# A replanned opening: ScalarE scales half of one attention unit, fillers move to free banks, and a transposition passes four loads

## The chip, the cores and the metric

The program runs on one core of a Trainium2 chip. The metric is the device time of one execution in microseconds (us), as the median of several runs. The engines are named as the profile names them: PE (TensorE, matmuls; PEld its weight loads), DVE (VectorE), ACT (ScalarE), POOL (GpSimd) and SP (SyncE, which here only issues transfers). "PEq" or "SPq" is the part of an engine that issues.

## The reference

Retention attention, then a two-layer feed-forward network with an ELU between the layers. There is no routing, although the weights are called moe.

```python
# q, k, v: (8 batches, 8 heads, 576 rows, 64), float32
scores = scale * np.matmul(q, k.transpose(0, 1, 3, 2))          # scale = 1/8
gamma = 1.0 - 2.0 ** (-5.0 - np.arange(H))
Dmat = np.where(rel >= 0, gamma[:, None, None] ** rel, 0.0)     # rel = row - column
attn = np.matmul(scores * Dmat, v)
x = attn.transpose(0, 2, 1, 3).reshape(4608, 512)               # heads side by side
h = x @ w_in                                                    # (512, 2048)
g = np.where(h > 0.0, h, np.exp(np.minimum(h, 0.0)) - 1.0)
out = g @ w_out                                                 # (2048, 512), float32 out
```

The decay is split into a factor for each query row (gamma to the power of its position, with the scale) and one for each key row (gamma to minus its position). So q and k are multiplied by small tables first, and the scores need only a mask of zeros and ones.

## The kernel before

**Units.** Rows 0 to 511 of every batch are cut into four units: two halves of 256 rows, each for heads 0 to 3 and for heads 4 to 7. Unit n is batch n // 4, so units 0 to 3 are batch 0, and unit 3 is its second half of rows with heads 4 to 7. Rows 512 to 575 of four batches at a time form a tail unit. A unit goes through these operations, which carry the names below in the code:

- `ldq`, `ldk`, `ldv`: loads of 256 KB, issued by SP (L422). From unit 8 on each is two loads of 128 KB (`ldq0_10`: queries of unit 10, first half; L412).
- `cq`, `ck` (L494): scaling of queries or keys by their table, with a cast to bf16, in two halves each. In a name like `ck13` the first digit is the half and the rest is the unit: second half of the keys of unit 3. `cv` (L545) casts the values.
- `T` and `cp` (L558, L564): PE transposes the scaled queries, then the keys, into PSUM, and ACT or DVE copies them out. From unit 7 on a transposing transfer from SP does this instead: `tr` (L602), which waits for the scaling of its unit.
- `sc`, `mask`: score matmuls, then the mask on DVE (L937; L931 from unit 8). `st`, `mid`, `end`, `bm`, `be`: the state (keys times values), running sums of it and their block-diagonal forms (L803 to L834), which later units of the batch read. `iv`: the unit's output, from states and from masked scores. `xc` copies it out as transposed tokens `xt` (L993). From unit 5 on one step `S` does the output of the unit or pair before and the scores and states of the next; `Sout7` is the output of unit 7 alone.

**Feed-forward.** Tokens are taken in blocks of 256 (blocks 0 to 5), later of 512. `F1_b_p` is a step of 8 matmuls of block b with w_in into one PSUM bank; then `ex` (Exp on ACT, L1145), `md` (max with 0 on ACT or DVE, L1153 or L1155) and `g` (on DVE, L1160) make the ELU, and `g` lets go of the bank. `F2_b_i_c` multiplies with w_out, over several steps into one bank, which `oc` (L1200) copies out after the last of them. There are six such banks (tag `f`) and two more for the scores. States and outputs of the units take banks from the same six.

**Weights.** w_in and w_out come in four pieces each, `wi0` to `wi3` and `wo0` to `wo3` (L471, L479), issued by POOL, which casts them to bf16 on the way. SP and POOL issue into two queues that share the 16 DMA engines. The loads of unit 4 are held back: a small memset of POOL into the buffer of its queries (`hold4`, L431) stands behind `wi0`, and `ldq4` waits for it.

**Order.** The order of all operations is not written out. At build time a planner (`Plan.run`) plays the program through with a cost for each operation on each engine it may run on, a rank, the dependencies and the numbers of buffers, and gives each engine one list, which then runs in that order. Constants steer it: `ON` fixes an operation to an engine, `RANKS` shifts a rank, `LAG` is an extra delay that the planner gives to transfers in a stretch of the opening. Where it finds PE idle in the first 50 us, the emitting loop at the end puts matmuls on a tile of zeros ahead of the next operation (fillers, L1341 to L1354), into that operation's own bank; ahead of a `T` they are transposes.

Of the kernel before, what the change touches and what calls it, by code (L numbers as in the profile page):

```python
# [11 lines left out]
FP32 = mybir.dt.float32  # L12
# [5 lines left out]
P = 128  # L18
# [6 lines left out]
class Op:  # L25


    def __init__(self, name, cost, deps, emit, rank, take=(), use=(), banks=(), dma=None, after=None):
        self.name, self.cost, self.emit, self.rank = name, cost, emit, rank
        self.deps = [d for d in deps if d is not None]  # L30
        self.turn = [] if after is None else [after]
        self.take, self.use, self.banks, self.dma = take, [*use, *(t[1] for t in take)], banks, dma
        self.eng = self.start = self.end = self.done = None
        self.slot, self.waits, self.at, self.side = {}, [], 0.0, False


class Plan:
# [30 lines left out]
    def run(self, began):  # L68
# [4 lines left out]
        bank, lanes = {}, {"SP": 0, "POOL": 0, "ACT": 0}  # L73
        wire = {"SP": [], "POOL": [], "ACT": []}
        free, order, events = dict(began), [], []
        ready, lack, next_of = {e: [] for e in began}, {}, {}
        for op in self.ops:
            lack[op] = len(op.deps) + len(op.turn)
# [48 lines left out]
        while len(order) < len(self.ops) or any(wire.values()) or events:  # L127
            again = True
            while again:
                again = False  # L130
                for e in began:
                    if free[e] > now + 1e-9:
                        continue
                    best = pick(e, now)
                    if best is None:
                        continue
                    _, op, got = best
                    for o in op.cost:
                        ready[o].remove(op)
                    cost = op.cost[e]  # L140
                    pay = cost[0] if isinstance(cost, tuple) else cost
                    if op.side and e in BESIDE and now + 0.15 < busy.get(BESIDE[e][0], 0.0):
                        pay += BESIDE[e][1]
                    if op.side:
                        busy[e] = now + pay
                    op.eng, op.start, op.end = e, now, now + pay - (LAP[e] if op.dma is None else 0.0)
                    op.done = None
                    op.waits = [*op.deps, *(bank[b] for b in op.banks if b in bank and bank[b].eng != e)]
                    for b in op.banks:
                        bank[b] = op  # L150
                    op.slot = {}
                    for key, (cls, n) in got.items():
                        if self.slots[cls][n] is not None:
                            op.waits += self.users[self.slots[cls][n]]
                        self.slots[cls][n], op.slot[key] = key, n
                    free[e] = op.end
                    heapq.heappush(events, (op.end, next(count), None))
                    if op.dma is None:
                        heapq.heappush(events, (op.end + HOP[e], next(count), op))
                    else:  # L160
                        lanes[e] += 1
                        enter = now + (op.dma[2] if len(op.dma) > 2 else ENTER)
                        heapq.heappush(events, (enter, next(count), None))
                        wire[e].append([enter, op.dma[0], op, False])
                    order.append(op)
                    met(op, "begun")
                    again = True
            heads = {e: w[0] for e, w in wire.items() if w and w[0][0] <= now + 1e-9}
            big = [e for e, h in heads.items() if h[3] and len(h[2].dma) > 2]
            heads = {e: h for e, h in heads.items() if h[3] or big in ([], [e])}  # L170
            for h in heads.values():
                h[3] = True
            turn = {e: h[2].dma[0] / h[2].dma[1] for e, h in heads.items()}
            rate = {e: turn[e] / sum(turn.values()) for e in heads}
            step = min([h[1] / rate[e] for e, h in heads.items()], default=1e9)
            assert events or heads, [o.name for o in self.ops if o not in set(order)][:20]
            if events:
                step = min(step, events[0][0] - now)
            step = max(step, 0.0)
            now += step  # L180
            for e, h in heads.items():
                h[1] -= step * rate[e]
                if h[1] < 1e-6:
                    wire[e].pop(0)
                    lanes[e] -= 1
                    heapq.heappush(events, (now + LEAVE + (LAG if LAG_AT < now < LAG_TO else 0.0), next(count), h[2]))
            while events and events[0][0] <= now + 1e-9:
                _, _, op = heapq.heappop(events)
                if op is not None:
                    finish(op, now)  # L190
# [3 lines left out]
ENTER, LEAVE = 1.25, 0.55  # L194
PIECE = 4.3
SEQ = "q0 k0 v0 q1 k1 v1 q2 k2 v2 q3 k3 v3"
LAG, LAG_AT, LAG_TO = 1.5, 11.3, 46.0


LEAD = 64  # L200
HOLD = {4: "wi0"}
RANKS = {}
TOGETHER = 1
EARLY = 5
LOOSE = True
# [3 lines left out]
POOL0 = 3.6  # L209
MERGE = {}  # L210
FROM = (8.96, 10.28, 13.13, 15.23, 17.0, 17.0, 17.44, 17.82)
ON = {'mid1': 'DVE', 'be2': 'DVE', 'md_1_0': 'ACT', 'xc1_2': 'DVE', 'cv0': 'DVE', 'md_1_1': 'ACT', 'cq12': 'DVE'}
DIRECT = True
PAIR = 8
FAR = 8
# [26 lines left out]
def kernel(  # L242
# [32 lines left out]
    def mm(*a, **kw):  # L275
        return pin(nc.tensor.matmul(*a, **kw))  # L276
# [209 lines left out]
    def scaled(it, i, e, cost):  # L486
        n = it.n
        key, raw = ("qkn", n), ("rq" + "qk"[i], n)
        g = ((far_q, far_k) if it.far else (gq, gk))[i]
        g = g[:, 2 * it.T + e, 4 * it.w : 4 * it.w + 4].unsqueeze(2).to_broadcast([P, 4, D])  # L490

        def emit(op):
            dst = by_head(n)[:, i, :, e] if it.far else tiles[key][:, i, e]
            pin(alu[op.eng].tensor_tensor(dst, tiles[raw][:, :, e], g, ALU.mult))  # L494

        first = not hasattr(it, "cq")
        if first:
            it.cq = {}
        ready = [it.ld["qk"[i], e], far_ready[0]] if it.far else [it.ld["qk"[i]]]
        op = add(f"c{'qk'[i]}{e}{n}", cost, ready, emit, it.rank,  # L500
                 take=[T("qkn", key, [P, 2, 2, 4, D], BF16)] if first else [], use=([] if first else [key]) + [raw],
                 after=it.cq0 if not first else None)
        if first:
            it.cq0 = op
        it.cq[i, e] = op
# [70 lines left out]
    def prepare(it, turn):  # L576
        n = it.n
        if it.early:
            qc, kc = {"DVE": 0.44, "POOL": 0.62}, {"POOL": 0.62, "DVE": 0.44}
            vc = {"ACT": 0.62, "POOL": 0.65, "DVE": (0.42, 0.3)}  # L580
        else:
            qc = kc = {"POOL": 0.64, "DVE": (0.6, 1.5)}
            vc = {"POOL": 0.65, "ACT": (0.62, 1.0)}
# [724 lines left out]
                        ffn2(blk, it, c, 4, rank + 8 * it + 2 * c, n0, n1)  # L1308

    for op in plan.ops:  # L1310
        op.side = len(op.cost) > 1 and op.name[:2] in ("cq", "ck", "ct", "cv", "bm", "be")
    named = {op.name: op for op in plan.ops}
    for op, name in holds:
        op.deps.append(named[name])
# [5 lines left out]
    for name, e in ON.items():  # L1320
        if name in named and e in named[name].cost:
            named[name].cost = {e: named[name].cost[e]}
    for name, shift in RANKS.items():
        if name in named:
            named[name].rank += shift
# [2 lines left out]
        PRINT(order)  # L1328
        return

    last = 1.3
    for op in order:
        for cls, key, shape, dt in op.take:
            pool = psum if cls in ("f", "sc") else sbuf
            if cls == "z":
# [2 lines left out]
                tiles[key] = put_aside(cls, op.slot[key], shape)  # L1338
            else:
                tiles[key] = pool.tile(shape, dt, name=cls, tag=f"{cls}{op.slot[key]}")  # L1340
        if op.eng == "PE":  # L1341
            gap = op.start - last if op.start < 50 and op.take else 0.0
            if gap > 0:
                spot = tiles[op.take[0][1]]
                left = int(gap * 0.8 / (0.107 if op.start < 7.0 else 0.056))
                while left > 0:
                    if op.name.startswith("T"):
                        wide = 1
                        pin(nc.tensor.transpose(spot[:, left % 4], zero[:, :P], ident))
                    else:  # L1350
                        wide = min(left, 4)
                        mm((spot if len(spot.shape) == 2 else spot[:, 0])[:, : wide * P], zero[:, :P],
                           zero[:, : wide * P], start=True, stop=True)
                    left -= wide  # L1354
            last = op.end
        op.emit(op)


# [31 lines left out]
```

## Time and profile before

| | |
|---|---|
| Three runs | 298.35, 298.99, 299.23 us; median 298.99 |
| The profiled execution | 299.29 us, of which the span from the first instruction to the last is 297.6 |
| PE busy | 291.7 us, 98% of the span |
| ACT, DVE, POOL busy | 195.1, 179.7, 136.5 us |
| First matmul of the feed-forward | at 18.91 us |
| First use of queries, keys and values of unit 4 by POOL | at 30.77, 34.33 and 37.99 us |
| First matmul of step `S7` | at 58.35 us |

Times of single instructions are counted from the start of the span. An engine runs its list in order, so an instruction that waits holds up all that stands behind it.

### The profile page before, as it was taken

The page shows a single profiled execution, that of the slowest core. Times are in us where ns is not written, and L with a number is a line of the kernel's source. Part 1 is how long each engine was busy: PE and PEld are TensorE (multiplying, and loading weights), DVE is VectorE, ACT ScalarE, POOL GpSimd, SP SyncE. Part 2 cuts the span into 40 slices and gives each one's busy share as a digit, 9 for nine tenths or more (in the row PEclk, how much of TensorE's full clock was granted, in tenths as well). Part 3 has the DMA queues.
Part 4 walks back from the last instruction along what each step waited for, and adds up shares of the span by engine and source line. Part 5 has one row for each costly group of instructions (what it writes and reads, how often), then busy time and mean ns, then how long its engine had stood idle before and what let it go on. Part 6 is the DMA issues. An engine that isn't in the chain of part 4 may idle for free.

```text
span 297.6 us, 8887 instructions
## 1 busy us (share of the span) xinstructions
PE 291.7 (98%) x3560; PEld 164.4 (55%) x3560; DVE 179.7 (60%) x323; ACT 195.1 (66%) x383; POOL 136.5 (46%) x257
## 2 busy tenths in 40 slices
PE   7999999999999999999999999999999999999996
PEld 3678746867776664545545454545444544444445
DVE  5999935838755849697756556666550169643300
ACT  2449823859768758778696868676772289777512
POOL 5880379956856755666534558542444000000000
PEclk9999999999999999999999999999999999999999
DMA  7999999999999999999999999996497410011132
GB/s 207 260 206 204 216 280 217 219 174 200 193 194 187 196 189 204 193 237 200 208 222 298 208 219 203 196 189 161 103 169 172 90 39 1 0 39 35 35 106 73
DMA packets 142010, 50.14 MB, mean 168 GB/s; under 512 B 120720, under 2 KB 137488, under 8 KB 141968
## 3 DMA queue, kind: packets, MB, share of 16 engines
q1 hardware_dynamic: 137744, 45.37, 78.3%
q0 software_dynamic: 4224, 4.19, 8.6%
q8 instruction: 28, 0.46, 0.7%
q14 instruction: 14, 0.11, 0.1%
HBM read 36.70 MB, written 9.44 MB: 155 GB/s over the span
## 4 chain that ended last, share of the span: by engine, by line
PE 86%; DMA 7%; POOL 3%; DVE 2%; SPq 1%; issue 0%; ACT 0%; ACTq 0%
PE f L276 84%; DMA rv<-in_v_dram 7%; PE sc L276 2%; POOL w_out_sb L479 1%; DVE pt L937 1%; SPq L422 1%; POOL w_in_sb L471 1%; POOL s_end L820 0%; POOL qkn L494 0%; DVE qkn L494 0%; PE f L558 0%; DVE s_end L820 0%; DVE s_mid L834 0%; POOL s_mid L820 0%; POOL vn L545 0%
## 5 line engine op out<-in xcount | busy, mean ns | idle before, releaser
L276 PE MATMUL f<-w_out_sb,g 128*128 128x512 bf16 (+2 forms) x608 | 141.1, 368 | 0.0
L276 PE MATMUL f<-xt,w_in_sb 128*128 128x256 bf16 (+1 forms) x768 | 138.2, 326 | 0.0
L1160 DVE SCALAR_TENSOR_TENSOR g<-e,f 128x512 bf16<-128x512 f32 x144 | 95.9, 684 | 69.0 <-ACT f L1153 53.2
L1145 ACT ACTIVATE e<-f 128x512 f32<-128x512 f32 x144 | 84.8, 597 | 33.7 <-PE f L276 25.7
L276 PEld LDWEIGHTS <-w_in_sb 128*128 128x128 bf16 x768 | 74.7, 98 | 53.5 <-DVE xt L988 0.4
L276 PEld LDWEIGHTS <-g 128*128 128x128 bf16 x608 | 56.6, 98 | 57.9
L1153 ACT ACTIVATE f<-f 128x512 f32<-128x512 f32 x116 | 68.5, 593 | 0.0
L494 POOL TENSOR_TENSOR qkn<-rqk,far_q 128x256 bf16<-128x256 f32 x48 | 28.9, 614 | 9.2 <-DMA rqk<-in_q_dram 9.0
L494 POOL TENSOR_TENSOR qkn<-rqk,far_k 128x256 bf16<-128x256 f32 x48 | 29.0, 616 | 7.6 <-DMA rqk<-in_k_dram 7.2
L1200 ACT COPY ot<-f 128x512 f32<-128x512 f32 (+2 forms) x30 | 16.8, 560 | 19.9 <-PE f L276 19.9
L545 POOL CAST vn<-rv 128x512 bf16<-128x512 f32 x28 | 17.1, 612 | 21.7 <-DMA rv<-in_v_dram 16.6
L972 ACT CAST xt<-f 128x512 bf16<-128x512 f32 x24 | 12.9, 589 | 16.1 <-PE f L276 16.1
L877 POOL CAST y<-mid 64x256 bf16<-64x256 f32 x36 | 14.3, 401 | 19.8 <-DVE mid L862 10.4
L1155 DVE TENSOR_SCALAR f<-f 128x512 f32<-128x512 f32 x28 | 19.4, 694 | 1.0 <-ACT e L1145 0.7
L931 DVE TENSOR_TENSOR pt<-sc,mask_t 128x1024 bf16<-128x1024 f32 x12 | 14.6, 1220 | 2.4 <-PE sc L276 2.4
L618 POOL TENSOR_TENSOR aside<-aside,gq 128x256 bf16<-128x256 f32 x16 | 9.4, 614 | 11.3 <-DMA aside<-in_k_dram 11.2
L494 POOL TENSOR_TENSOR qkn<-rqk,gq 128x256 bf16<-128x256 f32 x13 | 8.1, 633 | 12.3 <-DMA rqk<-in_q_dram 12.3
L877 ACT CAST y<-mid 64x256 bf16<-64x256 f32 x30 | 11.6, 402 | 2.1 <-DVE mid L860 1.0
L862 DVE TENSOR_TENSOR mid<-f,mid 128x256 f32<-128x256 f32 x24 | 10.2, 424 | 2.8 <-PE f L276 0.5
L276 PE MATMUL f<-pt,vn 64*64 64x64 bf16 (+1 forms) x512 | 11.5, 202 | 0.2 <-DVE pt L937 0.2
L993 ACT CAST xt<-f 128x256 bf16<-128x256 f32 x10 | 4.2, 452 | 10.8 <-PE f L276 10.8
L937 DVE TENSOR_TENSOR pt<-sc,mask 128x1024 bf16<-128x1024 f32 x8 | 9.8, 1220 | 2.2 <-PE sc L276 2.1
(92 smaller groups left out, 172.7 us busy)
## 6 DMA issues: line engine op xcount, KB each, us to landing
rqk<-in_q_dram SPq DMA_DIRECT2D x48, 128.0 KB, 3.9
rqk<-in_k_dram SPq DMA_DIRECT2D x48, 128.0 KB, 3.5
rv<-in_v_dram SPq DMA_DIRECT2D x48, 128.0 KB, 3.4
out_dram<-ot SPq DMA_DIRECT2D x18, 256.0 KB, 3.5
out_dram<-ot SPq DMA_DIRECT2D x19, 128.0 KB, 2.4
rqk<-in_q_dram SPq DMA_DIRECT2D x8, 256.0 KB, 6.8
rqk<-in_k_dram SPq DMA_DIRECT2D x8, 256.0 KB, 5.8
rv<-in_v_dram SPq DMA_DIRECT2D x8, 256.0 KB, 5.9
```

Source lines behind the costliest of these rows:

```text
L276: return pin(nc.tensor.matmul(*a, **kw))
L494: pin(alu[op.eng].tensor_tensor(dst, tiles[raw][:, :, e], g, ALU.mult))
L545: pin(copy[op.eng](tiles["vn", n], tiles["rv", n]))
L877: pin(copy[op.eng](dst, tiles[key][j * D : (j + 1) * D]))
L931: pin(nc.vector.tensor_tensor(tiles[it.pt].rearrange("p i h n -> p (i h n)")[:, : 2 * w * C].rearrange("p (i x n) -> p i x n", i=2, n=C), ...
L937: pin(nc.vector.tensor_tensor(tiles["pt", n].rearrange("p i h n -> p (i h) n"), tiles[it.sc].rearrange("p i (h n) -> p (i h) n", h=2), mas ...
L972: pin(copy[op.eng](by_block(it.xt)[:, 2 * it.T + c], tiles[xkey, c].rearrange("p (h n) -> p h n", n=P)))
L1145: pin(nc.scalar.activation(tiles[ekey], tiles[hkey], AF.Exp))
L1153: pin(nc.scalar.activation(ph, ph, AF.Relu))
L1155: pin(nc.vector.tensor_scalar_max(ph, ph, 0.0))
L1160: pin(nc.vector.scalar_tensor_tensor(tiles[gkey], tiles[ekey], -1.0, tiles[hkey], ALU.add, ALU.min))
L1200: pin(copy[op.eng](tiles[okey][:, :cols], tiles[pkey][:, :cols]))
```

## The change

Nothing that is computed changes. In the opening ACT takes four operations of unit 3, and some of the planner's rules and constants are changed, so that the lists of all engines differ in places.

- `cq13` and `ck13`, on POOL before, run on ACT, as four instructions each, one per head (a multiplication by a factor per partition). `ck03` goes from DVE to POOL, `cp(3, 0)` and `xc0_3` from DVE to ACT, `be3` from POOL to DVE, `md_0_1` from ACT to DVE.
- POOL's list is then: `bm2`, `ck03`, `wi3`, `wo0` to `wo3`, `hold4`. Before it was: `bm2`, `cq13`, `wi3`, `ck13`, `wo0` to `wo3`, `be3`, `hold4`.
- PE's list in the opening is: `T(3, 0)`, `T(3, 1)`, `iv2`, `sc3`, `st3`, first feed-forward step. Before: `T(3, 0)`, `iv2`, `T(3, 1)`, `st3`, `sc3`, first feed-forward step.
- Fillers go into whichever of the six banks has been free longest, ahead of any idle stretch that is planned, and never as transposes: 23 matmuls of up to 512 columns, 65 instructions before.
- `ldq0_10` may not go before `tr7`. SP's list there is: `ldv1_9`, `tr7`, the four loads of queries and keys of unit 10, `tr8`. Before: `ldv1_9`, those four loads, `tr7`, two loads of values and one of unit 11, `tr8`.
- PE's list from 56 us on: `S7` stands ahead of `F1_2_7`, and the last step `F2_2_0_3` of its bank stands behind `F1_3_3`; before it stood ahead of `F1_3_0`. `md_3_1` goes from ACT to DVE, ahead of `mask8`. Before `F1_3_4`, both lists hold the same steps.
- Later, neighbours change places in a few spots, and about 35 small operations change between ACT, DVE and POOL.

```diff
@@ Plan.run
                     if op.side and e in BESIDE and now + 0.15 < busy.get(BESIDE[e][0], 0.0):
-                        pay += BESIDE[e][1]
-                    if op.side:
-                        busy[e] = now + pay
+                        pay = max(pay, busy["POOL"] - now + 0.3) if e == "DVE" else pay + BESIDE[e][1]
+                    if op.side or e == "POOL" and op.dma is not None:
+                        busy[e] = now + (pay if op.side else 0.45)
...
+                    if e == "PE" and now < 50 and now > last + 0.01 and not op.name.startswith("F"):
+                        free_f = [(self.freed.get(old, 0.0), n, self.users.get(old, [])) for n, old in enumerate(self.slots["f"])
+                                  if old is None or self.left[old] == 0]
+                        if free_f:
+                            t, n, old = min(free_f, key=lambda f: f[:2])
+                            op.fill = n, max(0.0, now - max(last, t + 0.05)), old
+                    if e == "PE":
+                        last = op.end
@@ constants
-LAG, LAG_AT, LAG_TO = 1.5, 11.3, 46.0
+LAG, LAG_AT, LAG_TO = 0.6, 11.3, 46.0
+FILL = 0.8
+AFTER = {"ldq0_10": "tr7"}
-RANKS = {}
+RANKS = {"be2": 60, "be3": 60}
-ON = {'mid1': 'DVE', 'be2': 'DVE', 'md_1_0': 'ACT', 'xc1_2': 'DVE', 'cv0': 'DVE', 'md_1_1': 'ACT', 'cq12': 'DVE'}
+ON = {'ck13': 'ACT', 'cq13': 'ACT', 'mid1': 'DVE', 'md_1_0': 'ACT', 'xc1_2': 'DVE', 'cv0': 'DVE', 'md_1_1': 'ACT', 'cq12': 'DVE'}
@@ scaled
-            pin(alu[op.eng].tensor_tensor(dst, tiles[raw][:, :, e], g, ALU.mult))
+            if op.eng != "ACT":
+                pin(alu[op.eng].tensor_tensor(dst, tiles[raw][:, :, e], g, ALU.mult))
+                return
+            for h in range(4):
+                pin(nc.scalar.mul(dst[:, h], tiles[raw][:, h, e], g[:, h, :1]))
@@ prepare
-            qc, kc = {"DVE": 0.44, "POOL": 0.62}, {"POOL": 0.62, "DVE": 0.44}
+            qc = kc = {"DVE": 0.44, "POOL": 0.62, "ACT": (0.8, 9.0)}
@@ before the planner runs
-        op.side = len(op.cost) > 1 and op.name[:2] in ("cq", "ck", "ct", "cv", "bm", "be")
+        op.side = len(op.cost) > 1 and op.name[:2] in ("cq", "ck", "ct", "cv", "be")
+    for name, first in AFTER.items():
+        for one in (first if isinstance(first, tuple) else (first,)):
+            named[name].turn.append(named[one])
@@ the emitting loop
+        if op.fill:
+            left = int(op.fill[1] * FILL / (0.107 if op.start < 7.0 else 0.056))
+            if left:
+                spot = psum.tile([P, 512], FP32, name="f", tag=f"f{op.fill[0]}")
+            while left > 0:
+                wide = min(left, 4)
+                mm(spot[:, : wide * P], zero[:, :P], zero[:, : wide * P], start=True, stop=True)
+                left -= wide
...
-        if op.eng == "PE":
-            gap = op.start - last if op.start < 50 and op.take else 0.0
-            if gap > 0:
-                spot = tiles[op.take[0][1]]
-                left = int(gap * 0.8 / (0.107 if op.start < 7.0 else 0.056))
-                while left > 0:
-                    if op.name.startswith("T"):
-                        wide = 1
-                        pin(nc.tensor.transpose(spot[:, left % 4], zero[:, :P], ident))
...
```

More of the change, by code (lines that the diff above doesn't have):

```diff
@@ L34, in __init__ @@
         self.slot, self.waits, self.at, self.side = {}, [], 0.0, False
+        self.fill = None
 class Plan:
@@ L75, in run @@
         free, order, events = dict(began), [], []
+        last = began["PE"]
         ready, lack, next_of = {e: [] for e in began}, {}, {}
@@ L1329 @@
         return
-    last = 1.3
     for op in order:
+        if op.fill:
[6 more added lines that the diff above has]
+                left -= wide
         for cls, key, shape, dt in op.take:
@@ L1340 @@
                 tiles[key] = pool.tile(shape, dt, name=cls, tag=f"{cls}{op.slot[key]}")
-        if op.eng == "PE":
-            gap = op.start - last if op.start < 50 and op.take else 0.0
-            if gap > 0:
-                spot = tiles[op.take[0][1]]
-                left = int(gap * 0.8 / (0.107 if op.start < 7.0 else 0.056))
-                while left > 0:
-                    if op.name.startswith("T"):
-                        wide = 1
-                        pin(nc.tensor.transpose(spot[:, left % 4], zero[:, :P], ident))
[L1350 to L1355, printed above, removed]
         op.emit(op)
```

## The prediction

> **What bounds the kernel now.** I read the first page, then the chain in order of time, then the timelines of PE, ACT, POOL and DVE around each edit, then the landings of the weights.
>
> ```profile
> span 297.6 us, 8887 instructions
> ...
> PE 291.7 (98%) x3560; PEld 164.4 (55%) x3560; DVE 179.7 (60%) x323; ACT 195.1 (66%) x383; POOL 136.5 (46%) x257
> ...
> PE   7999999999999999999999999999999999999996
> ...
> PEclk9999999999999999999999999999999999999999
> ```
>
> PE is full from 18.91 us, where the feed-forward begins, so only two things can move the end: when PE starts its dense list, and whether a step in that list has to wait. The chain, merged in order of time, names one outside wait after the opening:
>
> ```profile
> 17.71 3.00 POOL w_out_sb L479 x4
> 20.70 0.64 POOL s_end L820
> 21.35 0.05 POOL rqk L431
> 21.39 0.02 issue
> 21.41 0.37 SPq L422
> ...
> 22.37 15.56 DMA rv<-in_v_dram
> 37.94 0.05 issue
> 37.99 0.62 POOL vn L545
> ```
>
> The values of unit 4 are loaded after POOL has issued `wo0` to `wo3`, run `be3` and `hold4`; they take 15.6 us, and PE's step `st4` starts at 38.65 behind their cast. PE's own timeline shows how close unit 4 is: its queries are scaled from 30.77 for 1.19 us, and the transposition that needs them starts at 31.99.
>
> ```profile
> 31.99 0.39 PE L558 MATMUL f<-ident,qkn 128*128 128x128 bf16 x4
> ...
> 38.65 0.32 PE L276 MATMUL f<-vn,qkn 64*64 64x64 bf16 x16 [0.18 <-POOL vn L545]
> ```
>
> The landings of w_in, then of w_out, by their lines:
>
> ```profile
> DMA to landing us min/median/max: 8.0/8.9/9.2
> ```
> ```profile
> DMA to landing us min/median/max: 11.5/15.8/20.2
> ```
>
> With issues at 9.7 to 16.2 and 17.7 to 19.9, w_in's pieces land from 17.7 to 25.4, 2.55 us apart, and w_out's from 29.2 to 40.1, 3.65 apart: the loads of unit 4 and after take their share of the wire then.
>
> **Change 1, the opening: about 0.92 us earlier.** ACT stands idle before 17.21 for 3.17 us:
>
> ```profile
> 17.21 0.45 ACT L993 CAST xt<-f 128x256 bf16<-128x256 f32 x1 [3.17 <-PE f L276]
> ```
>
> The two scalings go there as four instructions each. No row has this form. The nearest are the Exp tables, 0.28 to 0.32 us each with starts 0.21 to 0.23 apart: 4 x 0.22 + 0.1 = 0.98 for a half. The copy of 128x128 from PSUM, 0.27, would give about 0.8; four without any overlap 1.3. I take 0.98. `cq13` then runs from 14.05 to 15.0 and `ck13` to 16.0, while `ck03` takes `cq13`'s old place on POOL, 15.65 to 16.27 (0.62). So `T(3, 1)` starts at 16.3 instead of 17.40. Behind it: `iv2` 0.65, `sc3` 0.35. `st3` needs the values of unit 3, which by the trace land at 16.98; cast 0.61 gives 17.6, `st3` 0.25, and the first feed-forward step starts at 17.9 instead of 18.91. `wi0`, landed at 17.77, just allows that. `iv3` needs mask (1.22), `mid`, `end` (0.2 to 0.3 each as they overlap) and `bm3` 0.42 after `sc3`: about 19.92 against 20.84. From here PE is 0.92 early. Even at 1.3 per half ACT ends at 16.7, 0.4 late for `T(3, 1)`, and the gain is about 0.6.
>
> The page ScalarE: Activation LUTs of the Trainium skill, section Rules for kernel authors, advises VectorE over ScalarE for a multiplication, and that speaks against this edit: DVE does the half in 0.41 us. Here DVE has no idle stretch and ACT has, so by the trace the slower engine costs nothing.
>
> `be3` moves to DVE, 0.42 us beside POOL's issues up to 0.83 (the spread of L820 on DVE), ahead of the first `g`; that `g` then starts near 20.2 to 20.6, still before its old 21.12. Fillers fill waits; 0 by that, or up to 0.2 if a run of zeros outlasts its wait, since the longest wait now has two 512-column matmuls (0.43) in place of 21 transposes (1.2).
>
> **Change 2, POOL's issues: unit 4 about 1.15 us earlier.** Between `wi3` (ends 17.01) and `hold4` POOL loses `ck13` and `be3`. `wo0` to `wo3` follow at once, 3.04 us, so `ldq4` issues near 20.25 instead of 21.41. Unit 4's loads land by 1.15 earlier if the queue's wait is a fixed one, and by nothing if the loads only enter the wire when a weight piece is done. With 1.15, POOL has the queries scaled at 30.8, PE wants them at 31.07, and `st4` starts at about 37.5. No wait is left here, nor a loss.
>
> **Change 3, what the earlier loads take from the weights: minus 0.42 us.** While loads share the wire, a w_out piece takes 3.65 us and not 2.55. Sharing that begins 1.15 earlier therefore moves the last piece by 1.15 x (3.65/2.55 - 1) = 0.5, from 40.1 to 40.6. The step that reads it first is eight matmuls into the row that starts at 40.76 with ten, that is at 41.2 (two matmuls are 0.43); it starts at 40.7, 0.5 early instead of 0.92 or more. The DMA: Bandwidth & Descriptors page of the Trainium skill, section Issuing engines are not separate DMA queues, says that transfers of all issuers run on the same 16 engines and interleave; the change of spacing from 2.55 to 3.65 agrees.
>
> **Change 4, the order from 56 us on: minus 0.5 us.** Before, `F2_2_0_3` closed its bank ahead of `F1_3_0`, and `oc` let it go. Now that bank stays open over four `F1` steps: one for it, two for the states of `S8`, three for `F1_3_1` to `F1_3_3`. All six are taken when PE comes to `F1_3_4`, which waits for `g_3_1`. DVE before:
>
> ```profile
> 66.56 0.69 DVE L1160 SCALAR_TENSOR_TENSOR g<-e,f 128x512 bf16<-128x512 f32 x1 [2.47 <-ACT f L1153]
> 67.16 1.22 DVE L931 TENSOR_TENSOR pt<-sc,mask_t 128x1024 bf16<-128x1024 f32 x1
> 68.30 0.41 DVE L862 TENSOR_TENSOR mid<-f,mid 128x256 f32<-128x256 f32 x1
> 68.63 0.68 DVE L1160 SCALAR_TENSOR_TENSOR g<-e,f 128x512 bf16<-128x512 f32 x1
> ```
>
> There `g_3_1` ends at 69.31, and PE did not need it. After, with PE 0.5 early, `F1_3_0` starts 0.5 + 0.87 before its old 64.36, at 63.0; its Exp (old 65.44) at 64.1, max, then `g_3_0` at 65.2; `md_3_1`, new on DVE, 0.69, from 65.8; `mask8` from 66.4 (its scores are ready at 66.2), `mid1_8` 67.55, `g_3_1` 67.9 to 68.55. PE, having the same steps behind it as before, is at `F1_3_4` at 68.60 - 0.5 = 68.1, and starts it at 68.6: the old time. The wait hangs on PE's own steps, so it stays about 0.5 for any head start.
>
> **Change 5, `tr7` ahead of four loads: 0.** It issues near 52.1 (behind `ldv1_9`, and the keys of unit 7 are scaled at 51.9) instead of 54.38. `S7`, now one step earlier, wants it at 57.47 - 0.5 = 57.0. In this trace `S7` started 3.97 us after `tr7`'s issue without a wait, so 56.1 suffices. The loads behind it are 1.3 us later with PE no later; their units are used from 65 us on. What moves between ACT, DVE and POOL later, and the neighbours exchanged, leave PE's sum the same: 0, bounds plus or minus 0.2.
>
> **The sum.** -0.92 + 0.42 + 0.5 = 0.0. The profiled execution has 299.29 us, 1.69 around its span, and stands 0.30 above the median of the three runs. So: 299.3 by that execution, 299.0 as a median.
>
> **Rivals.**
> - *The loads of unit 4 don't come earlier.* For: after 21.41 nothing of the SP queue moves on the wire until about 25.0 in the trace's packets, which is when the last w_in piece is through. Against: the ramp over the engines from there takes 1.2 us, w_in's end 2.4. Then PE waits for the queries until 31.95 and the 0.92 are gone there; with change 4 the time is +0.5, 299.5.
> - *The bank comes free in time.* For: the order `g_3_1` behind `mask8` costs only if ACT and DVE keep the rows' times; 0.5 is little. Against: six banks, counted above. Then -0.5, 298.5; with the weights in time as well -0.92 to -1.15, 298.0.
> - *`tr7` becomes the wait (slower).* The transpositions of this trace take 3.5 to 5.9 us to land, median 4.7. `S7` stands ahead of all PE work, so every landing over 4.9 us after issue is paid in full: at 5.9 PE starts `S7` at 58.0, +1.0, 300.0. Against it the 3.97 above.
> - *Nothing changes because PE was full anyway.* That is the forecast's number by another road: then the first feed-forward step would stay at 18.9.
>
> **Chances.** Forecast 0.50 (its own range 298.6 to 299.4); loads no earlier 0.18; bank in time 0.14; bank and weights both in time 0.06; `tr7` late 0.09; 0.03 for what I don't see. 0.3% of 299 is 0.9 us, about what a measurement of this kernel tells from no change. Faster by that needs bank and weights both in time, or a gain unseen: 0.10. Slower needs `tr7` or two of the losses together: 0.15. Same: 0.75. Range 298.0 to 300.2.
>
> **What would show it.** First feed-forward step at 17.9 (change 1); `ldq4` at 20.25 and its scaling at 29.6 (2); PE idle for some 0.5 us near 40.3 ahead of w_out's last piece (3); PE idle 0.5 us near 68 behind DVE L1160 (4); `S7` without a wait near 57 (5). A scaling of unit 4 still at 30.7, or no idle at 68, makes the sum wrong.

## The result and the profile after

The changed kernel takes 299.50 us (median of 22 runs, 298.39 to 300.54), the kernel before 298.90 (22 runs beside them, 298.19 to 299.43). The ratio is 1.0024, with a 95% interval of 1.0014 to 1.0033: 0.6 us slower. That lies inside the 0.3% that I had called "same", and inside the range, but I had forecast 299.0, no change at all. The profiled executions don't show the 0.6: 299.32 us after, 299.29 before, both with a span of 297.6. Where the 0.6 is, and why the two profiles hide it, is what the experiments had to find.

The page of the changed kernel has the same picture as before, PE at 98%:

```profile
span 297.6 us, 8805 instructions
...
PE 291.2 (98%) x3518; PEld 162.3 (55%) x3518; DVE 181.1 (61%) x323; ACT 197.9 (66%) x393; POOL 133.7 (45%) x253
```

ACT in the opening (timeline of ACT; columns: start, us, engine, line, operation). The two halves of unit 3 now stand where ACT was idle:

```profile
13.21 0.45 ACT L1009 CAST xt<-f 128x256 bf16<-128x256 f32 x1 [0.32 <-PE f L288]
13.52 1.05 ACT L510 ACTIVATE qkn<-rqk,gq 128x64 bf16<-128x64 f32 x4
14.48 1.05 ACT L510 ACTIVATE qkn<-rqk,gk 128x64 bf16<-128x64 f32 x4
15.55 0.58 ACT L580 COPY qkT<-f 128x512 bf16<-128x512 bf16 x1
```

A half takes 0.96 from start to start. The first feed-forward step starts at 17.75 in place of 18.91.

The chain that ended last up to 45 us (columns: start, us, what) no longer goes through the values of unit 4. It goes through the last piece of w_out:

```profile
16.62 2.19 POOL w_out_sb L491 x3
18.81 21.69 DMA w_out_sb<-in_moe_w_out_dram
40.50 0.04 issue
40.55 1.89 PE f L288 x8
```

PE's timeline at that place and at 68 us shows two new waits; the number in brackets is the idle time before the row, and its releaser:

```profile
38.97 0.61 PE L288 MATMUL f<-w_out_sb,g 128*128 128x512 bf16 x2
40.55 1.89 PE L288 MATMUL f<-w_out_sb,g 128*128 128x512 bf16 x8 [0.97 <-DMA w_out_sb<-in_moe_w_out_dram]
...
67.08 1.03 PE L288 MATMUL f<-w_out_sb,g 128*128 128x512 bf16 x4
68.49 1.05 PE L288 MATMUL f<-xt,w_in_sb 128*128 128x256 bf16 x8 [0.39 <-DVE g L1176]
```

The second is the bank that `F1_3_4` needs. DVE's timeline shows what stands ahead of `g_3_1`, which frees it:

```profile
65.69 0.69 DVE L1171 TENSOR_SCALAR f<-f 128x512 f32<-128x512 f32 x1
66.30 1.22 DVE L947 TENSOR_TENSOR pt<-sc,mask_t 128x1024 bf16<-128x1024 f32 x1
67.43 0.41 DVE L878 TENSOR_TENSOR mid<-f,mid 128x256 f32<-128x256 f32 x1
67.76 0.68 DVE L1176 SCALAR_TENSOR_TENSOR g<-e,f 128x512 bf16<-128x512 f32 x1
```

So each step of the prediction is there. What is missing is a reason for 0.6.

### The profile page after: what moved, and what is told of

The parts are those of the page before. It is cut to its first block, busy times and chain, and to the rows that moved or that the text cites. A ratio compares the mean times of both kernels' runs of the same rounds, so it can differ in the third digit from the quotient of the medians.

```text
span 297.6 us, 8805 instructions
## 1 busy us (share of the span) xinstructions
PE 291.2 (98%) x3518; PEld 162.3 (55%) x3518; DVE 181.1 (61%) x323; ACT 197.9 (66%) x393; POOL 133.7 (45%) x253
## 4 chain that ended last, share of the span: by engine, by line
PE 85%; DMA 7%; DVE 3%; POOL 2%; issue 1%; ACT 0%; ACTq 0%; DVEq 0%
PE f L288 83%; DMA w_out_sb<-in_moe_w_out_dram 7%; PE sc L288 2%; DVE pt L953 1%; POOL w_out_sb L491 1%; PE f L574 1%; POOL w_in_sb L483 1%; DVE g L1176 0%; DVE qkn L507 0%; DVE qkT L580 0%; DVE s_mid L850 0%; POOL s_mid L836 0%; POOL s_end L836 0%; DVE f L1171 0%; ACT e L1161 0%
## 5 line engine op out<-in xcount | busy, mean ns | idle before, releaser
L1169 ACT ACTIVATE f<-f 128x512 f32<-128x512 f32 x113 | 66.6, 592 | 0.0
L893 POOL CAST y<-mid 64x256 bf16<-64x256 f32 x33 | 12.8, 398 | 25.4 <-DVE mid L878 8.9
L988 ACT CAST xt<-f 128x512 bf16<-128x512 f32 x24 | 12.9, 589 | 15.1 <-PE f L288 15.1
L1171 DVE TENSOR_SCALAR f<-f 128x512 f32<-128x512 f32 x31 | 21.3, 694 | 2.5 <-ACT e L1161 2.4
L947 DVE TENSOR_TENSOR pt<-sc,mask_t 128x1024 bf16<-128x1024 f32 x12 | 14.6, 1219 | 3.2 <-PE sc L288 3.2
L893 ACT CAST y<-mid 64x256 bf16<-64x256 f32 x33 | 12.8, 402 | 1.8 <-DVE mid L878 0.9
L507 POOL TENSOR_TENSOR qkn<-rqk,gq 128x256 bf16<-128x256 f32 x12 | 7.4, 630 | 11.9 <-DMA rqk<-in_q_dram 11.9
L288 PE MATMUL f<-zero 128*128 128x512 bf16 (+3 forms) x30 | 9.2, 416 | 1.3 <-DVE zero L293 1.3
```

The lines of the kernel that those rows point to most:

```text
L893: pin(copy[op.eng](dst, tiles[key][j * D : (j + 1) * D]))
L947: pin(nc.vector.tensor_tensor(tiles[it.pt].rearrange("p i h n -> p (i h n)")[:, : 2 * w * C].rearrange("p (i x n) -> p i x n", i=2, n=C), ...
L988: pin(copy[op.eng](by_block(it.xt)[:, 2 * it.T + c], tiles[xkey, c].rearrange("p (h n) -> p h n", n=P)))
L1169: pin(nc.scalar.activation(ph, ph, AF.Relu))
L1171: pin(nc.vector.tensor_scalar_max(ph, ph, 0.0))
```

## The experiments

The kernels ran in four groups, each group on one chip beside runs of the kernel before, and a median is set against the median of before in the same group. The ratio and its interval are worked out over all the runs of both kernels, so the ratio is not that of the two medians. Theory W says that the end now hangs on the landing of the last piece of w_out, and on the bank; rival L that the later lists cost the 0.6; rival B that the bank swallows any lead. Two more theories, S (nostall) and O (before2), came up on the way.

To compare profiles I cut each into three stretches at two steps that all kernels have: from the first feed-forward step (`F1_0_0`) to the first use of the last piece of w_out (`F2_0_0_6`), from there to `F1_3_4`, and from there to the span's end.

| Profile | `F1_0_0` at | last piece lands | used at | stretch 1 | stretch 2 | stretch 3 | span |
|---|---|---|---|---|---|---|---|
| before, first | 18.91 | 40.15 | 41.21 | 22.29 | 27.39 | 228.98 | 297.6 |
| before2 | 18.60 | 39.18 | 40.42 | 21.82 | 27.40 | 229.04 | 296.9 |
| before3 | 17.98 | 39.76 | 39.80 | 21.83 | 27.40 | 228.77 | 296.0 |
| after, first | 17.75 | 40.50 | 40.55 | 22.80 | 27.94 | 229.12 | 297.6 |
| again | 18.56 | 41.08 | 41.12 | 22.57 | 27.95 | 229.81 | 298.9 |
| nostall | 19.24 | 39.67 | 40.90 | 21.66 | 27.95 | 229.05 | 297.9 |
| wo2 | 17.89 | 39.78 | 39.56 | 21.66 | 27.95 | 229.31 | 296.8 |
| bank | 17.74 | 39.78 | 39.83 | 22.09 | 27.39 | 230.06 | 297.3 |
| both | 17.75 | 40.14 | 39.42 | 21.66 | 27.40 | 229.96 | 296.8 |
| scale | 18.11 | 40.59 | 40.63 | 22.53 | 27.40 | 229.32 | 297.4 |
| late4 | 19.02 | 41.59 | 41.63 | 22.62 | 27.95 | 229.76 | 299.3 |
| no_tr7 | 17.86 | 40.60 | 40.64 | 22.79 | 27.40 | 229.02 | 297.1 |
| ver | 17.79 | 40.44 | 40.48 | 22.69 | 26.53 | 229.09 | 296.1 |
| ver_again | 18.00 | 40.11 | 40.53 | 22.53 | 26.53 | 228.93 | 296.0 |

(In wo2 and both the step doesn't read the last piece. In ver and ver_again one step of 0.86 us stands in stretch 1 instead of stretch 2.)

**again: the changed kernel, unedited.**

> The changed kernel itself, a second profile. Theory W (the last piece of w_out): in the profile of the changed kernel PE waits 1.14 us for that piece (landed 40.50, first use 40.55), so everything behind it starts when a transfer lands; the kernel before first uses it 1.06 us after its landing. W expects the first use again within 0.1 us of the landing, wherever the landing is (39.5 to 42), the step S7 moved by as much, and a time near 299.5 with single runs over 2 us apart. Rival L (the order and the small operations behind 70 us cost the 0.6): first use and S7 stay where they were within 0.1, and PE shows new idle behind 70 us.

Measured: 299.40 against 298.81, ratio 1.0022 (0.9997 to 1.0046). In its profile the piece lands at 41.08 and is used at 41.12, as W says. But two things were new. The values of unit 3 landed at 17.62 instead of 14.48, ACT's cast waited for them, and the feed-forward started 0.8 later:

```profile
15.86 0.59 ACT L580 COPY qkT<-f 128x512 bf16<-128x512 bf16 x1
17.64 0.62 ACT L561 CAST vn<-rv 128x512 bf16<-128x512 f32 x1 [1.19 <-DMA rv<-in_v_dram]
```

And at 91 us one cast of DVE took 2.65 us, where the first profile has 0.38. DVE's timeline of again:

```profile
90.90 0.29 DVE L893 CAST y<-mid 64x256 bf16<-64x256 f32 x1
91.22 2.65 DVE L893 CAST y<-end 64x256 bf16<-64x256 f32 x1
93.79 0.69 DVE L1171 TENSOR_SCALAR f<-f 128x512 f32<-128x512 f32 x1
```

POOL's timeline of again, over the same stretch:

```profile
91.03 0.42 POOL L893 CAST y<-end 64x256 bf16<-64x256 f32 x1
91.39 0.61 POOL L561 CAST vn<-rv 128x512 bf16<-128x512 f32 x1
91.97 1.18 POOL L507 TENSOR_TENSOR qkn<-rqk,far_q 128x256 bf16<-128x256 f32 x2
93.11 0.60 POOL L507 TENSOR_TENSOR qkn<-rqk,far_k 128x256 bf16<-128x256 f32 x1
```

And PE's, with the idle time behind DVE's late `g`:

```profile
93.67 1.03 PE L288 MATMUL f<-w_out_sb,g 128*128 128x512 bf16 x4
95.25 0.94 PE L288 MATMUL f<-xt,w_in_sb 128*128 128x256 bf16 x7 [0.56 <-DVE g L1176]
```

POOL ran without a pause from 91.03 to 93.71; the cast began inside that stretch and ended at 93.87. Stretch 3 is 229.81, 0.69 longer than in the first profile. So L has a share in such a run.

**wo2: the wait for the last landing taken away.**

```
-    mm(pm, g[...], w_out_sb[:, ft, n0:n1], ...)
+    mm(pm, g[...], w_out_sb[:, ft - 4 if blk == 0 and ft > 11 else ft, n0:n1], ...)
```

> Leaves out: in block 0 the steps that belong to the fourth piece of w_out multiply with the third piece, so the first 256 rows of the output are not the reference's; the work is the same, only the wait for the last landing is gone. W: the first of these steps starts at 39.4 in place of 40.55, PE is about 1.7 us ahead of the kernel before there, the scaling and casting of units 5 and 6 on POOL (which follow a landing at 39.45) take back 0.5 to 0.7 of the 1.1 by S6, the bank's wait at F1_3_4 keeps its 0.5; median 298.7 to 299.1, and single runs closer together than 2 us. Rival L: 299.4 to 299.6, all of what is won at 40 is lost again behind 70. Rival B (the bank at 68 us takes any lead): F1_3_4 starts at 68.5 as in the changed kernel, 299.5.

Measured: 298.89 against 298.81, ratio 1.0007 (0.9990 to 1.0025). PE's timeline of wo2 runs through at 39 us, ten matmuls in one row, and shows the bank's wait at 67.51:

```profile
39.11 2.33 PE L288 MATMUL f<-w_out_sb,g 128*128 128x512 bf16 x10
...
67.51 1.05 PE L288 MATMUL f<-xt,w_in_sb 128*128 128x256 bf16 x8 [0.39 <-DVE g L1176]
```

Stretch 1 is 21.66, so the wait in the first profile of after was 22.80 - 21.66 = 1.14. The median falls by 0.5 against again, where I had expected 0.4 to 0.8; but the two intervals overlap, so it is the profile, and not the times, that shows the wait gone. Units 5 and 6 took nothing of it back by S6: it started 1.0 earlier than in the first profile of after. The bank's wait is untouched by a PE 1.0 earlier: stretch 2 is 27.94 or 27.95 in all profiles that have it. B is wrong: the wait is a fixed amount, not a fixed time. That single runs would lie closer was a miss (298.19 to 301.23).

**bank: the old place of `F2_2_0_3`.**

```
-AFTER = {"ldq0_10": "tr7"}
+AFTER = {"ldq0_10": "tr7", "F1_3_0": "F2_2_0_3_0"}
```

> One constraint more: the last step of the bank, F2_2_0_3, goes ahead of F1_3_0 as in the kernel before; the lists are the same up to 62 us. W and B: no idle of PE at F1_3_4, which starts at 67.9 in place of 68.5; median 0.5 less, 299.0. L: 299.4 to 299.6, since some lists change again behind 75 us but the neighbours swapped there stay.

Measured: 300.04 (7 runs) against 298.81, ratio 1.0045 (1.0019 to 1.0071). PE goes through three steps at 65 us without a gap, and stretch 2 is 27.39. But the new constraint changed the planner's list at 237 us too: `F2_12_3_3` moved ahead of the output of unit 33, and nothing was left to cover the copy of that output (PE's timeline of bank at both places):

```profile
65.47 2.79 PE L288 MATMUL f<-xt,w_in_sb 128*128 128x256 bf16 x24
...
237.66 0.45 PE L288 MATMUL f<-pt,aside 64*64 64x64 bf16 x32
238.94 0.82 PE L288 MATMUL f<-xt,w_in_sb 128*128 128x512 bf16 x3 [0.84 <-DVE xt L1004]
```

That wait of 0.84 is most of the 0.94 by which stretch 3 is longer than in the first profile of after. The expected 0.5 is seen at its place and lost at another. The median is another 0.6 above again, which this profile (298.98 us) doesn't explain; with seven runs the interval still overlaps with that of the changed kernel (1.0014 to 1.0033), and it stays open.

**both: the two edits together.**

> wo2 and bank together; leaves out the same part of block 0 as wo2 does. W: the two prices add up, 298.1 to 298.5, that is 0.4 to 0.8 below the kernel before. B: 298.0, all of the lead of 1.2 gets through as soon as the bank is free. L: not under 299.0.

Measured: 298.64 against 298.81, ratio 0.9997 (0.9977 to 1.0017). Stretches 1 and 2 are both at their shortest (21.66 and 27.40); the same wait of 0.84, here at 238.44, stands against them. The expected 298.1 to 298.5 had not counted it, and was missed by 0.14.

**scale: the scaling on ACT alone, in the kernel before.**

```
-ON = {'mid1': 'DVE', ...
+ON = {'ck13': 'ACT', 'cq13': 'ACT', 'mid1': 'DVE', ...
```
(with the new branch of `scaled` and the cost for ACT; all other constants as before)

> The kernel before with the scalings of the second half of unit 3 on ACT and nothing else of the change: the old constants, the old fillers, the old list from 50 us on. W: the opening is as much earlier as in the changed kernel (first feed-forward step near 17.8, or near 18.4 where the values of unit 3 land late), ldq4 issues near 20, PE waits for the last piece of w_out where it comes to it early, and keeps about 0.65 of its lead; no wait for a bank at F1_3_4. Median 0.3 to 0.65 below the kernel before. Rival L (the loss lies in the later lists): the same, -0.3 to -0.65, since the later list is the old one. If the loss came with the early opening itself (the loads of unit 4 on the wire with the weights): 0.0 or above.

Measured: 299.26 against 298.81, ratio 1.0017 (1.0004 to 1.0031). This refutes W's number and L's: it is slower, the third case of the expectation. The opening is early (18.11), and so is the first load of unit 4 (issued at 19.36), and the last piece lands at 40.59 (PE's timeline of scale):

```profile
39.42 0.60 PE L276 MATMUL f<-w_out_sb,g 128*128 128x512 bf16 x2
40.63 1.24 PE L276 MATMUL f<-w_out_sb,g 128*128 128x512 bf16 x5 [0.60 <-DMA w_out_sb<-in_moe_w_out_dram]
```

So the edit that starts PE earlier also empties POOL's list earlier, and by that sends the loads of unit 4 out sooner, and PE finds the last weights later. The gain and its price come from one and the same move. Against before2 the opening gains 0.49, stretch 1 loses 0.71, and stretch 3, where PE's list is that of before, another 0.28 in small shifts that no run here explains.

**late4: those loads held back.**

```
-    pin(nc.gpsimd.memset(tiles[key][:, 0, 0, :1], 0.0))
+    for _ in range(3):
+        pin(nc.gpsimd.memset(tiles[key], 0.0))
```

> The changed kernel with three memsets of the whole buffer in hold4 in place of one column, so that the loads of unit 4 are issued later, by 1 to 2 us, with all lists the same. W: of each us that ldq4 is later, the last piece of w_out lands 0.3 earlier against wi0's landing (mean of the changed kernel and its three neighbours 23.0 us from landing to landing, the kernel before 22.4): 22.4 to 22.7, and PE's wait for it is smaller by that; st4 may wait for the values of unit 4 instead. Median 299.0 to 299.3. Rival (the loads take nothing from the weights): 23.0, and the time at or above 299.5 by what st4 waits.

Measured: 300.03 against 298.81, ratio 1.0048 (1.0028 to 1.0068). The hold was 1.75 us long (POOL's timeline of late4):

```profile
20.34 1.75 POOL L444 MEMSET rqk<- 128x512 f32 x3
```

From wi0's landing to that of the last piece it took 22.62. Sorted by when `ldq4` was issued after wi0's landing: 1.9 to 3.0 us in eight profiles of the changed opening (after, again, wo2, bank, both, no_tr7, ver, ver_again), with 22.7 to 23.4 to the last piece, mean 23.0; 3.15 here; 3.4 in nostall, where POOL was late in the opening, with 21.9; 3.2 to 4.2 in the three profiles of before, with 22.3 to 22.5. The kernel scale, which has the new opening with the old lists, fits as well: 2.5 and 23.7. So the landing does move with the loads, as expected, though with some scatter. What moves lies between the landings of wi0 and wi3: 7.7 to 7.9 in before, 7.0 in nostall, 8.0 here, 8.0 to 8.7 in the eight, 9.1 in scale. From wi3 to the last piece it is 14.6 to 15.1 in all of them. The time didn't follow: this profile has the late opening of again (values of unit 3 at 17.98) and again the cast of 2.65 us at 91. As a test of the time it says nothing.

**no_tr7: without the rule on `tr7`.**

```
-AFTER = {"ldq0_10": "tr7"}
+AFTER = {"F2_12_3_3_0": "Sout33"}
```

> The changed kernel without the rule that ldq0_10 waits for tr7 (and with F2_12_3_3 held behind the output of unit 33, as in both kernels). The planner then puts S7 behind F2_1_1_3 and F2_2_0_3 ahead of F1_3_0: the rule alone made change 4. W: tr7 issues 0.5 to 1.5 later, S7 does not wait, no bank's wait at F1_3_4, the wait for the last piece of w_out as in the changed kernel; median 298.7 to 299.0. If the rule was needed: S7 waits by 0.5 or more, 299.5.

Measured: 298.62 (298.27 to 299.00) against 298.81, ratio 0.9994 (0.9984 to 1.0004). Stretch 2 is back at 27.40, stretch 3 at 229.02, and PE's wait for the last piece is still there (the line that the edit adds only keeps `F2_12_3_3` where both kernels have it; PE's timeline of no_tr7):

```profile
39.08 0.61 PE L288 MATMUL f<-w_out_sb,g 128*128 128x512 bf16 x2
40.64 1.24 PE L288 MATMUL f<-w_out_sb,g 128*128 128x512 bf16 x5 [0.96 <-DMA w_out_sb<-in_moe_w_out_dram]
```

The interval ends below that of the changed kernel (1.0014 to 1.0033), so the loss goes with the rule: without it the kernel is not slower than before, although it still waits for the piece. So the order that costs 0.55 at 68 us is a consequence of one rule about a load at 52 us, which the prediction had priced at 0. Without the rule the planner itself moves `S7` back by two steps, `tr7` issues at 53.59, and `S7` doesn't wait.

**nostall: one cast moved from DVE to ACT.**

```
-ON = {'ck13': 'ACT', ...
+ON = {'b31_12': 'ACT', 'ck13': 'ACT', ...
```

> The changed kernel with one cast of 64x256 (b31_12, the last of unit 12's running sums) on ACT in place of DVE; every other entry of every list is the same. In the second profile of the changed kernel this cast took 2.65 us at 91.2 (0.38 in the first), ending as a chain of POOL operations ended, and PE lost 0.72 behind it. Theory S: the later DVE comes to this cast, the surer it falls into POOL's chain; so the runs whose opening is late pay a second time. S expects the runs over 300.2 gone, median 299.0 to 299.3, and in a profile no idle at F1_5_1. W alone: 299.4 to 299.6 with the same spread, the cast costs only what that one profile showed.

Measured: 299.19 against 298.65, ratio 1.0006 (0.9983 to 1.0029), 298.08 to 300.50. The profile has no long cast at 91, and stretch 3 is 229.05, as in the first profile of after, although the opening is the latest of all (19.24) and PE comes to `F1_5_0` at 92.56. Of the other profiles with the cast on DVE, the two that come there at 92.79 and 93.17 have the long cast (229.81, 229.76), the two at 91.10 and 92.18 have not. So a late run pays some 0.7 there: shown in two profiles. That it makes the difference of the medians isn't shown: one of 12 runs is still over 300.2, and of the runs of the kernel before beside it two came to 300.96 and 300.05.

**before2 and before3: the kernel before, two more profiles, of one execution each.**

> The kernel before, a second profile. Its first profile stands 0.4 above the median of its runs, and in it the values of unit 3 landed at 16.98 and PE waited 0.37 for them. Theory O: in most runs of the kernel before they land near 14.5, the feed-forward then starts near 18.55, PE comes to the last piece of w_out at 40.85 with the piece just landed, and the span is 297.1 to 297.2; so its two medians differ by 0.6 although the two first profiles have one span. If O is wrong: first step at 18.9 again, or at 18.55 with the span at 297.6.

> The kernel before, a third profile; O as in the second: the span follows the landing of the values of unit 3, 297.1 to 297.2 with 14.5, 297.5 to 297.6 with 17.

Measured: 298.56 us with a span of 296.9, and 297.77 with 296.0. O is right that the first profile was a late one and names the wrong cause. The values of unit 3 landed at 14.58 and 14.95 in these two and at 16.98 in the first, and yet `st3`, which reads them, started 0.89 or 0.90 after `T(3, 1)` in all three, and their cast stood 0.31 or 0.32 behind the copy ahead of it on ACT; so the landing doesn't set it. What differs is the whole opening (18.91, 18.60, 17.98), with the issue of its loads: that of the queries of unit 3 is at 7.51, 7.19 and 6.69. And the waits for unit 4 are in the first profile alone: stretch 1 is 22.29 there and 21.82 and 21.83 in the others. About half of that 0.47 (22.29 - 21.82) is the wait for its values, the one outside wait of my chain: from the row ahead of it `st4` starts after 1.65 (37.00 to 38.65) and in before2 after 1.40. The other half is a wait for its scaled keys inside the transposition ahead of `sc4`, which takes 0.60 instead of 0.39. PE's timeline of before (first profile):

```profile
35.26 0.60 PE L558 MATMUL f<-ident,qkn 128*128 128x128 bf16 x4
35.69 1.03 PE L276 MATMUL f<-w_out_sb,g 128*128 128x512 bf16 x4
```

In the other two PE's rows run through without a wait. PE's timeline of before2, there and at the last piece:

```profile
34.94 0.39 PE L558 MATMUL f<-ident,qkn 128*128 128x128 bf16 x4
35.16 1.03 PE L276 MATMUL f<-w_out_sb,g 128*128 128x512 bf16 x4
...
39.63 0.42 PE L276 MATMUL f<-pt,vn 64*64 64x128 bf16 x16
39.98 1.90 PE L276 MATMUL f<-w_out_sb,g 128*128 128x512 bf16 x8
```

The same of before3:

```profile
39.01 0.42 PE L276 MATMUL f<-pt,vn 64*64 64x128 bf16 x16
39.36 2.33 PE L276 MATMUL f<-w_out_sb,g 128*128 128x512 bf16 x10
```

**ver and ver_again: a version meant to beat both.** One step of block 1 on w_out goes ahead of the steps that need the last piece, and the two orders are put right:

```
+                    if c == 6:
+                        ffn2(seq[1], 0, 0, 4, rank + 11)
...
-                    for c in range(4):
+                    for c in range(int((i, it) == (1, 0)), 4):
...
-AFTER = {"ldq0_10": "tr7"}
+AFTER = {"ldq0_10": "tr7", "F1_3_0": "F2_2_0_3_0", "F2_12_3_3_0": "Sout33", "T(5, 0)": "F2_0_1_7_0"}
```

> A version meant to beat both: the changed kernel, with the first step of block 1 on w_out (F2_1_0_0, 0.86 us) ahead of the steps that need the last piece, F2_2_0_3 ahead of F1_3_0 again, and F2_12_3_3 behind the output of unit 33 as in both kernels (in the runs bank and both it stood ahead of it, and PE waited 1.18 us at 237 for the tokens of the tail). W: PE's wait for the last piece falls from about 1.1 to 0.3, no wait at F1_3_4, none at 237; the last steps 1.2 to 1.5 us ahead of the kernel before in a profile with an early opening; median 297.5 to 298.2. Rival L: 298.5 or more, with new idle between 70 and 230 us.

> The kernel of ver a second time, for its size: its first comparison had a median 0.8 below the kernel before and an interval from 0.9964 to 1.0009. W: PE comes to the last piece of w_out with one step more behind it, so the first of those steps again follows the landing by 0 to 0.4 while the step S5 behind them starts 0.8 earlier than it would, no wait at F1_3_4; median 297.8 to 298.3, ratio 0.997 to 0.9985. If the first comparison was luck: ratio 0.9995 or more.

Measured: 298.04 against 298.81, ratio 0.9987 (0.9964 to 1.0009), and 298.27 against 299.14, ratio 0.9985 (0.9965 to 1.0004). PE fills the wait with the step that doesn't need the piece (twelve matmuls in one row), and has no gap at 65 (PE's timeline of ver):

```profile
39.01 2.93 PE L288 MATMUL f<-w_out_sb,g 128*128 128x512 bf16 x12
...
65.25 2.79 PE L288 MATMUL f<-xt,w_in_sb 128*128 128x256 bf16 x24
```

Stretches 1 and 2 together are 49.22 and 49.06; before has 49.22 in its two undelayed profiles, the changed kernel 50.74, 50.52 and 49.61. So this version keeps the early opening. Both medians are 0.8 to 0.9 below before, twice, though each interval by itself just reaches 1.

## Why the prediction was right or wrong

The time came inside the range and the class was right, but the number was 0.5 too low, and the median lies 0.1 above the likeliest case's own range.

- **Change 1 (-0.92).** The mechanism was right: a half costs 0.96 (I had 0.98) and the first step started at 17.75 (17.9). The size against the first profile of before was 1.16. But that profile started late: the three of before have 18.91, 18.60 and 17.98, and the nine of the changed opening without the long hold 17.74 to 19.24 with a median of 17.86. The gain by medians is 0.74. The Trainium skill's advice for VectorE (ScalarE: Activation LUTs, Rules for kernel authors) was rightly put aside for ACT's own time; the scaling on ACT costs at another place, by what it lets POOL send.
- **Change 2.** `ldq4` was issued at 19.73 (20.25 predicted) and landed 2.7 earlier; the queries of unit 4 were scaled from 28.06 (29.6). The rival "loads no earlier" gave the time that came, 299.5, by a mechanism that did not happen. The packets in the traces settle it: the first of unit 4's came 3.5 to 3.8 us after the issue of `ldq4` in all 14 profiles, at 25.04 in the first of before and at 23.37 in the first of after, where the last piece of w_in landed only at 25.63. So here that wait hangs on the issue and not on the weights, as the forecast took it.
- **Change 3 (+0.42).** The piece landed at 40.50 (40.6 predicted) and its first use started at 40.55 (40.7). The place and the cause were right, and by the eight profiles under late4 the landing moves by 23.0 - 22.4 = 0.6 against wi0's (0.5 predicted). That 40.50 lies so near 40.6 is luck: the landing is anywhere from 39.78 to 41.08 in those eight. The sharing sets in while w_in's last pieces are still moving, not only among those of w_out: the last of w_in landed 3.09 after the one ahead of it, 2.52 before.
- **The step that failed** is the difference at this point: "0.5 early instead of 0.92 or more", taken from 41.21. In that 41.21 stood 0.47 of waiting for unit 4's keys and values, which the other two profiles of before don't have (I had read 0.18, the values alone), and an opening 0.3 to 0.9 later than theirs. Their first use is at 40.42 and 39.80. So the changed kernel, held by the landing at 40.55, is not early at all against a run of before without those delays. before2, with 298.56, is close to the medians of before; before3, with 297.77, is faster than any of the 22 runs beside the result. The term that was too small is that of change 3: 0.42 in the sum, against the 0.98 and 0.75 by which stretch 1 of the first two profiles of after is longer than that of before2. I saw that the profiled execution stood 0.30 above the median, and took the 0.30 off both kernels alike. It belongs to before alone: after's profiled execution stands 0.18 below its median.
- **Change 4 (+0.5).** Right: `F1_3_4` started at 68.49 (68.6), `g_3_1` at 67.76 (67.9). "It stays about 0.5 for any head start" is shown by stretch 2, 27.94 or 27.95 with the bank late and 27.39 or 27.40 without, whenever PE comes.
- **Change 5 (0).** `S7` had no wait (56.81), and `tr7` landed 3.52 after its issue. But the rule was not free: no_tr7 shows that change 4 comes from it. I had priced them as two changes.
- **Later swaps (0 ± 0.2).** Stretch 3 is 229.05, 229.12 and 229.31 in the three profiles of the changed list without the long cast, against 228.77 to 229.04: about 0.2. Not foreseen is the cast at 91 us, 0.7 in a late run.

Read in stretches, the 0.6 is this: -0.74 by medians for the opening; 0.98 for stretch 1 with its wait for the last piece in the first profile of after (22.80 against 21.82), less where the opening is late; 0.55 for the bank; some 0.2 later. -0.74 + 0.98 + 0.55 + 0.2 = 1.0; with stretch 1 of again (22.57 - 21.82 = 0.75) it is 0.8, and nostall, which opened late, had no wait at all. The measured 0.6 is near these, but openings vary by over 1 us between runs, so a sum from so few profiles is no closer than some tenths. What the times themselves show is that the loss goes with the rule on `tr7` (no_tr7); that the early opening and the later landing cancel to within some tenths is read from profiles.

## What to carry to other kernels

Before a sum is made against one profiled execution, see which of its waits other executions share: here the one outside wait of the chain was not in the next two profiles, and the offset to the median belonged to one kernel and not to both. Where an edit shortens an engine's list, look at what that engine issues behind it: POOL's earlier loads cost the weights what the shorter opening had won, and only work that doesn't need the late piece, put ahead of it, let PE keep the lead. A rule about one load made a planner reorder steps that run some 10 us later and cost 0.55, so a planner's whole list has to be compared after each constant.

## What the runs showed of the hardware

- A DVE cast of 64x256 from f32 to bf16 took 2.65 us at 91 us in again and late4 instead of 0.29 to 0.43, when it began inside an unbroken stretch of POOL operations, and ended 0.15 after that stretch did. Such casts took 2.56 at 166 to 167 us in four profiles (after, again, nostall, late4), and 2.65 at 193 and 194 us in both and no_tr7, with PE not waiting for them there. At 193 us it took 0.95 in the first profile of before and in bank: there POOL paused after one operation, and the cast ended 0.15 after that one; in all ten places the distance is 0.15 or 0.16. The Trainium skill, SBUF — State Buffer, section SBUF: two separate sides, says that VectorE in a 2-port mode and GpSimd share one pair of ports by an exclusive lock that an instruction holds to its end. If the cast runs in such a mode, the row agrees, and adds that several POOL operations in a row can pass ahead of the one that waits. That the port is the cause is argued from the times alone.
- The first packets of a load that SP issued while pieces of the weights were on their way came 3.5 to 3.8 us after its issue (`ldq4`, 14 profiles, issues from 19.36 to 22.12).
- The opening of one and the same program varies by about 1 us: the first feed-forward step at 17.98 to 18.91 in three profiles of before. In the changed lists the values of unit 3 landed at 14.2 to 14.5 in some profiles and at 16.1 to 18.0 in others, with issues at 8.9 to 9.8. What decides it was not tried.
